# Two gate products of the first chunk moved into the prologue of a fused attention and GLU kernel, its last keys in halves, its statistics divided anew

## The chip, the core and the metric

The kernel runs on one core of a Trainium2 chip. The metric is the device time of one execution in microseconds (us), the median of three runs. The core's engines work through lists of instructions of their own, in order, and wait for each other with semaphores: TensorE (PE in the profile, PEld its weight loads), VectorE (DVE), ScalarE (ACT), GpSimd (POOL), and SyncE (SP), which here only issues transfers (DMA). PE writes its results into PSUM, a memory of eight banks of 2 KB for each of 128 partitions; all else is in SBUF.

## The reference

The input x has 2048 tokens of 640 values; weights and data are bf16. Two branches share the layer norm of x:

```python
xn = (x - mean) / sqrt(var + 1e-5)
# attention, 32 heads of 20
q, k, v = split(xn @ wqkv)
s = softmax(q @ k.T * 20 ** -0.5) @ v @ wo
# gated linear unit, F = 1728
h = sigmoid(xn @ w_gate) * (xn @ w_up)
g = silu(h @ w_down)
out = x + s * g
```

## The kernel before, in words

The queries are cut into four chunks of 512 tokens (`QC`), the heads into eight groups of four (`GH`); a block is one group with one chunk of queries. The program has two stages, and in both the Python code works out an order of instructions ahead of time from assumed costs, by a clock of its own (`t` in the first, `now` in the second). The chip then runs each engine's list in that order; nothing is reordered there.

**The prologue** (L199 to L401) loads 16 tiles of 128 tokens of x and makes from them the transposed, normalised input `xnT`, and the keys, queries and values that the first block needs. Its pieces are `Step` objects with a cost on each engine that may run them, predecessors, and a key: at each time an engine takes the ready step with the largest length of work behind it (`order()`) less its `late`. For each tile:

- `s_stats` takes mean and variance, on DVE (two statistics instructions and one to join them) or on ACT (two passes with sums, L269 and L270); `ACT_STATS` lists the tiles that ACT has, here eight. `X_AT` is the time from which a tile is assumed to be there.
- `s_rstd` takes the inverse root on POOL, for `RH` tiles at once; for tiles of ACT it also corrects the mean (L279).
- `s_xn` normalises on DVE, `s_tr` transposes on PE in five pieces into a PSUM buffer `tp`, and `s_ev` copies that into `xnT` on ACT or DVE, whichever is free (L295).

For each chunk, `s_k` multiplies the keys of the first head group into the PSUM bank `pk`, `s_kmax` takes their largest absolute value per row on DVE, `s_kt` copies them out. `s_q`, `s_abs`, `s_bound` and `s_qev` make the queries of the first block: an upper bound of each row's scores, from the maxima of all four chunks, is subtracted by a matmul (`q_bound`), so that the exponentials need no running maximum. So the first scores wait for the maximum of the last chunk's keys. `s_v` and `s_vev` make values for the first two chunks (`NVP`). Where PE has nothing ready, it gets a scrap matmul (L398) on a tile `busy` and a bank `scrap` of its own, whose result nobody reads.

**The main stage** (L1160 to L1500) simulates PE, ACT and DVE in steps of 0.02 us and emits what they would take next. Score tiles of 128 keys by 512 queries are filled by PE (`score_mm`, L889). ACT turns most into exponentials (`exp_act` over `act_imm`, L82: pairs into `pt`, single ones into `px`). DVE does the others with integer arithmetic: it reads the scores into `iv` (L1327) and makes three passes over four such tiles into `pb` (L1019, L1022, L1025); a DVE tile goes through PE's second product twice. `oacc` (L926) sums the weighted values. Everything else is an `Item` that fills gaps: keys, queries and values for later groups, then `glu_items`, in order, which hold the whole GLU. For each chunk `mk_gu` makes 14 column tiles: a gate product, tanh on ACT (L82, output `tnh`), an up product, and on DVE (tanh + 1) × up into `hT` (L690). The last column tile is half as wide and is handled apart. Then `mk_down` multiplies `hT` with `wd`. All these PE products go by `cols` (L471), four matmuls on four column strips of the array at once.

**Transfers.** The order of SP's transfers isn't written out: they are put where their buffers come free. `load_wgu(c, k2)` (L425) loads gate and up weights of two column tiles, 320 KB each, into one of two buffers. The first such load, the output weights `wo` and the down weights `wd` stand in the code at the start of the main stage (L1161 to L1170), with two small POOL memsets of `wd` and `hT`. The pools `late` (`wd`, `wo`, `hT`) and `w2` (the weights `wgu` and all buffers of the main stage) are opened after the prologue's pool `lp` is closed, on the same memory. The small weights of the second head group (`load_wst`, spread on POOL by L128) are loaded during the prologue.

## Time and profile before

The median of three runs is 803.62 us (802.97 to 803.87). The profiled execution took 803.38 us, of which its span, first to last instruction, is 801.6; the mean granted clock of TensorE was 0.997.

| Stretch, us | length | PE busy | DVE busy | ACT busy | POOL busy | what |
|---|---|---|---|---|---|---|
| 0 to 4 | 4 | 2.69 | 0.79 | 2.36 | 3.10 | first tiles land, scrap matmuls |
| 4 to 8 | 4 | 1.31 | 2.86 | 3.94 | 3.55 | statistics |
| 8 to 12 | 4 | 3.61 | 3.70 | 2.56 | 3.58 | first transposes |
| 16 to 18 | 2 | 2.00 | 2.00 | 1.97 | 1.56 | middle of the prologue |
| 24 to 26 | 2 | 1.99 | 1.49 | 1.51 | 0 | last transposes |
| 26 to 28 | 2 | 1.83 | 0.85 | 0.34 | 0 | last keys |
| 28 to 30 | 2 | 1.01 | 1.22 | 0.51 | 0.95 | bound, first scores |
| 30 to 34 | 4 | 3.10 | 2.64 | 3.84 | 0.99 | main stage begins |
| 130 to 330 | 200 | 196.87 | 196.98 | 199.89 | 15.69 | middle of the main stage |
| 790 to 796 | 6 | 6.00 | 3.84 | 0.74 | 1.63 | last output tiles |

DMA is busy until 14.2 us, then nearly idle to 29, and busy again to 42 (0.96 to 1.08 of the 16 engines).

How to read a row of the profile: in a list of instructions in order of time, the columns are start, duration (of all that the line merges), engine, source line, operation, output <- inputs, shapes, count; in square brackets the idle time of the engine before it, and whose end it waited for by the profile. A matmul's duration includes its way through the array, so rows that follow each other overlap: what one costs is read from start to start. The scrap matmuls count as busy PE.

### The profile page before, as it was taken

What the parts mean: (1) busy time and instruction counts of PE and PEld (TensorE: products, weight loads), DVE (VectorE), ACT (ScalarE), POOL (GpSimd) and SP (SyncE); (2) the same over time, 40 slices, a digit from 0 to 9 for tenths busy, and PEclk for the clock granted to TensorE, in tenths of its full rate; (3) what the DMA queues carried; (4) which work ended last, traced back from release to release, by engine and by line L of the source; (5) the groups of instructions that cost most, each with busy time, mean ns of one, the idle gap of its engine ahead of it and who ended that gap; (6) DMA issues with size and microseconds to landing.
All of it is one profiled execution on the core that took longest, in us unless ns stands there. A gap on an engine that the chain in (4) does not pass through costs nothing.

```text
span 801.6 us, 25395 instructions
## 1 busy us (share of the span) xinstructions
PE 778.0 (97%) x10462; PEld 283.8 (35%) x10466; DVE 770.2 (96%) x1239; ACT 781.2 (97%) x991; POOL 107.4 (13%) x219
## 2 busy tenths in 40 slices
PE   7899999999999999999999999999999999999996
PEld 5523233333433323334332332334333333333333
DVE  7798999999999999989999999999999999999996
ACT  8799999999999999999999999999999999999993
POOL 7200000000000000000000010000000100502425
PEclk9999999999999999999999999999999999999999
DMA  5541213123122323222113132222311332331421
GB/s 162 147 117 48 70 40 86 53 67 80 46 69 61 78 67 100 51 60 68 49 47 97 50 86 76 80 75 60 96 40 58 91 90 53 105 104 34 131 62 62
DMA packets 91851, 60.47 MB, mean 75 GB/s; under 512 B 34891, under 2 KB 85627, under 8 KB 91735
## 3 DMA queue, kind: packets, MB, share of 16 engines
q1 hardware_dynamic: 91447, 58.52, 26.2%
q8 instruction: 82, 1.34, 0.7%
q14 instruction: 34, 0.28, 0.1%
q10 hardware_dynamic: 288, 0.33, 0.1%
HBM read 45.18 MB, written 11.09 MB: 70 GB/s over the span
## 4 chain that ended last, share of the span: by engine, by line
PE 47%; ACT 39%; DVE 6%; issue 5%; DMA 1%; POOL 1%; DVEq 0%; ACTq 0%; POOLq 0%; SPq 0%
ACT pt L82 31%; PE bk L473 20%; PE scA L889 14%; PE oacc L926 10%; ACT px L82 4%; DVE iv L1327 2%; ACT tnh L82 2%; DVE pb L1025 1%; PE bk L889 1%; ACT td L82 1%; DVE pb L1022 1%; PE tp L292 1%; DVE pb L1019 0%; DMA lt<-ld 0%; ACT aq L173 0%
## 5 line engine op out<-in xcount | busy, mean ns | idle before, releaser
L82 ACT ACTIVATE pt<-scA 128x1024 bf16<-128x1024 f32 (+1 forms) x709 | 707.8, 1186 | 1.2 <-PE scA L889 0.5
L1327 DVE TENSOR_SCALAR iv<-bk 128x512 int16<-128x512 f32 x500 | 331.5, 680 | 12.1 <-PE bk L889 9.6
L889 PE MATMUL scA<-q,kT 32*128 32x512 bf16 x1412 | 275.8, 382 | 8.7 <-ACT pt L82 3.3
L889 PE MATMUL bk<-q,kT 32*128 32x512 bf16 x636 | 207.3, 383 | 0.2 <-DVE iv L1327 0.2
L889 PEld LDWEIGHTS <-kT 32*128 32x128 bf16 x2048 | 88.4, 91 | 262.0 <-issue 250.7
L926 PE MATMUL oacc<-pt,v 128*21 128x512 bf16 x1412 | 178.6, 381 | 1.0 <-ACT pt L82 0.7
L926 PE MATMUL oacc<-pb,v 128*21 128x512 bf16 x1000 | 161.4, 382 | 0.0
L473 PE MATMUL bk<-xnT,wgu 128*32 128x512 bf16 x2160 | 157.3, 383 | 0.5 <-DVE iv L1327 0.2
L1025 DVE TENSOR_TENSOR pb<-iv,pb 128x2048 bf16<-128x2048 bf16 x125 | 152.0, 1216 | 0.7
L979 POOL TENSOR_TENSOR on_bf<-on,rl 128x128 bf16<-128x128 f32 x116 | 54.4, 473 | 626.7 <-DVE iv L1327 149.1
L82 ACT ACTIVATE px<-bk 128x512 bf16<-128x512 f32 x136 | 101.0, 760 | 1.7 <-POOL hT L1169 1.6
L1019 DVE TENSOR_SCALAR pb<-iv 128x2048 int16<-128x2048 int16 x125 | 86.9, 695 | 0.4
L473 PE MATMUL bk<-wd,hT 128*32 128x320 bf16 x1792 | 87.0, 302 | 0.1
L1022 DVE TENSOR_SCALAR pb<-iv 128x2048 int16<-128x2048 int16 x125 | 86.2, 690 | 0.0
L926 PEld LDWEIGHTS <-v 128*21 128x21 bf16 x2548 | 54.0, 91 | 76.2 <-issue 53.4
L473 PEld LDWEIGHTS <-wgu 128*32 128x32 bf16 x2160 | 44.5, 95 | 64.3 <-issue 45.9
L473 PEld LDWEIGHTS <-hT 128*32 128x32 bf16 x1792 | 37.5, 95 | 38.2 <-issue 32.7
L473 PE MATMUL bk<-xnT,wu 128*32 128x512 bf16 x640 | 48.4, 383 | 0.6 <-DVE iv L1327 0.2
L926 PE MATMUL oacc<-px,v 128*21 128x512 bf16 x136 | 46.7, 381 | 0.0
L82 ACT ACTIVATE tnh<-bk 128x512 bf16<-128x512 f32 (+1 forms) x56 | 43.2, 772 | 0.1
L690 DVE SCALAR_TENSOR_TENSOR hT<-tnh,bk 128x512 bf16<-128x512 bf16 x52 | 35.3, 679 | 1.0 <-PE bk L889 0.3
L800 POOL TENSOR_TENSOR xnT<-otmp,xnT 128x160 bf16<-128x160 f32 x48 | 28.2, 607 | 40.6 <-PE bk L889 15.9
(118 smaller groups left out, 410.5 us busy)
## 6 DMA issues: line engine op xcount, KB each, us to landing
rl<-rd SPq DMA_DIRECT2D x124, 64.0 KB
wgu<-in_B_w_gate_dram SPq DMA_DIRECT2D x24, 320.0 KB
wgu<-in_B_w_up_dram SPq DMA_DIRECT2D x24, 320.0 KB
gq_dram<-gqs SPq DMA_DIRECT2D x24, 160.0 KB
xnT<-gq_dram SPq DMA_DIRECT2D x12, 320.0 KB
xt<-in_A_x_dram SPq DMA_DIRECT2D x16, 160.0 KB
xnT<-in_A_x_dram SPq DMA_DIRECT2D x16, 160.0 KB
out_dram<-xnT SPq DMA_DIRECT2D x14, 160.0 KB
```

What stands on the lines that cost most here:

```text
L82: return nc.scalar.add_instruction(mybir.InstActivation(func=func, name=nc.get_next_instruction_name(), engine=ENG.Activation, ins=[nc.sca ...
L292: nc.tensor.transpose(out=tps[k][:, kd, :], in_=xns[k][:, kd * P:(kd + 1) * P], identity=ident)
L473: nc.tensor.matmul(out[j:j + 32, :], lhsT=lhsT[:, j:j + 32], rhs=rhs, start=start, stop=stop, tile_position=(0, j), skip_group_check=True)
L690: return nc.vector.scalar_tensor_tensor(out=hT[0:fs, kf, :], in0=st["t"][0:fs, :], scalar=1.0, in1=st["u"][0:fs, :], op0=ALU.add, op1=ALU. ...
L800: add = nc.gpsimd.tensor_tensor(out=xr[:, cs], in0=tmp[:, i * HD // 2:(i + 1) * HD // 2], in1=xr[:, cs], op=ALU.add)
L889: nc.tensor.matmul(dst, lhsT=kTs[gc_of(b)[0] % 2][32 * j:32 * j + 32, kt * P:(kt + 1) * P], rhs=qts[b % 3][32 * j:32 * j + 32, :], start=T ...
L926: nc.tensor.matmul(oacc[32 * j:32 * j + DH + 1, :], lhsT=lhsT, rhs=u["src"], start=first, stop=last, tile_position=(0, 32 * j), skip_group ...
L979: ins = nc.gpsimd.tensor_tensor(out=on_bf[:, cs], in0=on[:, cs], in1=rl[:, cs], op=ALU.mult)
L1019: ins = nc.vector.tensor_scalar(out=pb[:, 0, :, :].bitcast(I16), in0=iv, scalar1=0x7F80, scalar2=1, op0=ALU.bitwise_and, op1=ALU.bitwise_or)
L1022: ins = nc.vector.tensor_scalar(out=pb[:, 1, :, :].bitcast(I16), in0=iv, scalar1=0x007F, scalar2=0x3F00, op0=ALU.bitwise_and, op1=ALU.bitw ...
L1025: ins = nc.vector.tensor_tensor(out=pb[:, 1, :, :], in0=iv.bitcast(BF16), in1=pb[:, 1, :, :], op=ALU.mult)
L1327: beat(nc.vector.tensor_scalar(out=d["iv"][:, j, :], in0=bank[bk], scalar1=B_OFF, scalar2=0.0, op0=ALU.add, op1=ALU.max))
```

## The change

Five things change, nearly all in the prologue.

1. **Gates of the first chunk.** The gate products of the first two column tiles (`NGP = 2`; `NHP = 0`: no product with the up part) are multiplied in the prologue, with full-width matmuls in three steps each, from planned time 14.0 (`G_AT`) on and with low rank (`L_G`); tanh of them goes straight into `hT[:, 0]` and `hT[:, 1]`. In the main stage `mk_gu` returns only the up item for these two, and its DVE product reads `hT` in place.
2. **Weights and memory.** The pools `late` and a new `wg` (weights `wgu`, `tnh`, `gql`) are opened before the prologue. The first gate and up weights are loaded right behind the value weights, the second pair at the start of the main stage, and the load that the first up item started is left out.
3. **Last keys in two halves.** `KP` splits the key product and the maximum of the fourth chunk in 256 columns each; the tile of maxima has room for eight, five are used.
4. **Statistics.** ACT keeps tiles 2, 4, 10 and 12; DVE has the other twelve. The offsets `L_*` of the ranks change, and `EARLY` adds to the rank of five single steps.
5. **PSUM and scrap.** Transposes have three buffers where they had four, values (with the gates and the scrap bank) share three where values had one and scrap one. Scrap matmuls stop at planned time 13.0 (`T_SCR`).

```diff
-    def k_max(g, c, src=None):
+    def k_max(g, c, src=None, n=NQC):
         if not mk_n.setdefault(g, []):
-            mks[g] = wk.tile([P, NQC], FP32, tag="mk4", bufs=2, name="mk4")
+            mks[g] = wk.tile([P, 2 * NQC], FP32, tag="mk4", bufs=2, name="mk4")
...
-            nc.vector.tensor_reduce(out=mk, in_=mks[g], axis=AXISX, op=ALU.max)
+            nc.vector.tensor_reduce(out=mk, in_=mks[g][:, 0:n], axis=AXISX, op=ALU.max)
...
+    late = ctx.enter_context(tc.tile_pool(name="late", bufs=1))
+    wg = ctx.enter_context(tc.tile_pool(name="wg", bufs=2))
+    wd = late.tile([P, NFT, D], BF16, name="wd", tag="wd")
+    wo = late.tile([P, KD, D], BF16, name="wo")
+    hT = late.tile([P, NFT, QC], BF16, name="hT")
...
+    NGP, NHP = 2, 0
     NVP = 2
-    RH = 2
+    RH = (2, 2, 2, 2)
+    KP = [[(0, 4)], [(0, 4)], [(0, 4)], [(0, 2), (2, 4)]]
+    EARLY = {('stats', 15): 4.0, ('stats', 12): 2.0, ('ev', 6): -1.0, ('kt', 2): 4.0, ('k', 1, 0): 8.0}
...
-    L_ST, L_CH, L_K, L_V, L_Q = 4.0, 1.5, 10.0, 3.0, 2.0
-    ACT_STATS = (0, 2, 4, 7, 8, 10, 11, 12)
+    G_AT, L_G, NPV, T_SCR = 14.0, 11.0, 3, 13.0
+    L_ST, L_CH, L_K, L_V, L_Q = 3.0, 2.0, 7.0, 7.0, 0.5
+    ACT_STATS = (2, 4, 10, 12)
...
         wv0 = load_wv(0)
+        for k2 in range((NGP + 1) // 2):
+            load_wgu(0, k2)
...
-            tps[k] = psP.tile([P, KD, P], BF16, tag="tp", bufs=4, name="tp")
+            tps[k] = psP.tile([P, KD, P], BF16, tag="tp", bufs=3, name="tp")
...
-        def s_k(eng, c):
-            pks[c] = psP.tile([P, 512], FP32, tag="pk", bufs=1, name="psk")
-            k_mm(pks[c], 0, c)
+        def s_k(eng, c, lo, hi):
+            if lo == 0:
+                pks[c] = psP.tile([P, 512], FP32, tag="pk", bufs=1, name="psk")
+            q = slice(lo * P, hi * P)
+            for kd in range(KD):
+                nc.tensor.matmul(pks[c][:, q], lhsT=wslice(0, 1, kd), rhs=xnT[:, c, kd, q],
+                                 start=(kd == 0), stop=(kd == KD - 1))
...
+        def s_gu(eng, kf, i, lo):
+            if lo == 0:
+                gus[(kf, i)] = psP.tile([P, 512], FP32, tag="pv", bufs=NPV, name="psg")
+            for kd in range(lo, min(KD, lo + 2)):
+                nc.tensor.matmul(gus[(kf, i)], lhsT=wgu_tiles[(0, kf // 2)][:, i, kd, kf % 2 * P:kf % 2 * P + P],
+                                 rhs=xnT[:, 0, kd, :], start=(kd == 0), stop=(kd == KD - 1))
+
+        def s_th(eng, kf):
+            act_imm(hT[:, kf, :], gus[(kf, 0)], ACT.Tanh, 0.5)
...
+            for lo, hi in KP[c]:
+                km = Step(s_k, (c, lo, hi), {"PE": 0.04 + 0.27 * (hi - lo)}, (spread, *evs[4 * c + lo:4 * c + hi], *mine[-1:]),
+                          take=None if lo else "pk", late=L_CH * c + L_K)
+                mine.append(km)
+                kms.append(Step(s_kmax, (c, lo, hi), {"DVE": 0.08 + 0.14 * (hi - lo)}, (km, *kms[-1:]), late=L_CH * c))
...
+        hs = []
+        for kf in range(NGP):
+            for i in range(2 if kf < NHP else 1):
+                for lo in range(0, KD, 2):
+                    g = Step(s_gu, (kf, i, lo), {"PE": 0.44 if lo < 4 else 0.22}, (*evs[0:4], *hs[-1:]), G_AT, take=None if lo else "pv", late=L_G)
+                    hs.append(g)
+                if i == 0:
+                    th = Step(s_th, (kf,), {"ACT": 0.48}, (g,), give="pv", late=L_G)
...
-        scrap = psP.tile([P, 512], FP32, tag="scrap", bufs=1, name="scrap")
+        scrap = psP.tile([P, 512], FP32, tag="pv", bufs=NPV, name="scrap")
...
-                    s = max(can, key=lambda s: s.order() - s.late)
+                    s = max(can, key=lambda s: s.order() - s.late + EARLY.get((s.f.__name__[2:],) + s.args[0:2], 0.0))
...
-                elif e == "PE" and engs[e] <= t:
+                elif e == "PE" and engs[e] <= t < T_SCR:
...
-            if ko == 0:
+            if ko == 0 and not early:
...
+            t = hT[:, kf, :] if early else st["t"]
+            return nc.vector.scalar_tensor_tensor(out=hT[0:fs, kf, :], in0=t[0:fs, :], scalar=1.0,
                                                   in1=st["u"][0:fs, :], op0=ALU.add, op1=ALU.mult)
...
+        return pair[1:] if early else pair
...
-        load_wgu(0, 0)
+        load_wgu(0, (NGP + 1) // 2)
```

## The prediction

> **What bounds the kernel now.** I read the page first (span, engine shares), then the busy time by stage, then the prologue in order of time with the waits in it, and the granted clock there microsecond by microsecond.
>
> ```profile
> span 801.6 us, 25395 instructions
> PE 778.0 (97%) x10462; PEld 283.8 (35%) x10466; DVE 770.2 (96%) x1239; ACT 781.2 (97%) x991; POOL 107.4 (13%) x219
> ```
>
> Three engines look equally full. The stages tell them apart (columns: stretch, length, busy time of PE, PEld, DVE, ACT, POOL, clock, DMA):
>
> ```profile
> 24.00:26.00 2.00, 1.99 (x28) 1.73 (x27) 1.49 (x3) 1.51 (x3) 0.00 (x0) 1.00 0.00 0
> 26.00:28.00 2.00, 1.83 (x12) 0.97 (x10) 0.85 (x2) 0.34 (x2) 0.00 (x0) 1.00 0.00 0
> 28.00:30.00 2.00, 1.01 (x10) 0.36 (x10) 1.22 (x3) 0.51 (x1) 0.95 (x2) 1.00 0.00 0
> 130.00:330.00 200.00, 196.87 (x2636) 68.90 (x2625) 196.98 (x314) 199.89 (x251) 15.69 (x35) 1.00 0.26 70
> 330.00:530.00 200.00, 196.81 (x2636) 68.44 (x2636) 194.42 (x306) 199.89 (x249) 14.44 (x32) 1.00 0.24 66
> ```
>
> From 42 us on ACT is busy 99.9% of the time, DVE and PE a little less: the main stage lasts as long as ACT's list, and DVE shares the exponentials. Before it ACT is nearly empty from 26 to 30 us. What it waits for is a chain (start, duration, what):
>
> ```profile
> 24.82 0.88 DVE L295 COPY xnT<-tp 128x640 bf16<-128x640 bf16 x2
> 25.82 1.24 PE L142 MATMUL psk<-xnT,wqk 128*128 128x512 bf16 x5
> 27.10 0.69 DVE L158 TENSOR_REDUCE mk<-psk 128x1 f32<-128x512 f32 x1 [1.40 <-PE psk L142]
> 27.83 0.16 DVE L162 TENSOR_REDUCE mk<-mk 128x1 f32<-128x4 f32 x1
> 28.02 0.25 DVE L163 TENSOR_SCALAR md<-esum,mk 128x128 bf16<-128x128 bf16 x1
> 28.76 0.69 DVE L180 TENSOR_SCALAR q<-psq 128x512 bf16<-128x512 f32 x1 [0.48 <-PE psq L177]
> 30.16 0.60 ACT L82 ACTIVATE px<-bk 128x512 bf16<-128x512 f32 x1 [1.64 <-POOL hT L1169]
> ```
>
> The last copy out of PSUM ends at 25.70, the maximum of the last keys starts at 27.10, and the first exponential at 30.16. The bracket on that last line names POOL, but DVE's first read of scores starts at 30.12, so the scores (started at 29.60) explain 30.16 too. Before 25.70, DVE works from 3.58 on with 1.59 us of named waits: it is the fuller engine of the prologue.
>
> **The change part by part.** Durations are start to start, since rows overlap.
>
> *Main stage.* Two gate products and two tanh leave. ACT: a tanh starts at 44.40, the next instruction at 44.88, and 52.43 to 52.90: 0.48 each, 0.95 together. If DVE cannot take less, ACT's list shortens by 0.95. If the split is rebalanced: eight exponentials of 1024 take 52.43 − 44.88 = 7.55, so 0.47 a score tile on ACT; on DVE a tile costs 0.60 (from 45.37 to 45.97, one 512-wide read of PSUM to the next) and a quarter of three passes (0.60 + 0.60 + 1.13), 1.18. Rates 2.12 and 0.85 a us: 0.95 × 2.12 / 2.97 = 0.68. PE: 40 matmuls in groups of four that run together; twenty ran from 42.72 to 43.92, the start of the next fill, 1.2 each gate. A freed PE also feeds DVE, which waited 10 us for score tiles over the stage (group of that read: 10.2 before it). So 0.68 at least, 2.4 if PE alone were the bound, 0.68 being nearest to ACT's 99.9%; I take 1.0. Any new order of the whole stage may move ±1.
>
> *Last keys in two halves.* The first half (tiles 12 and 13) is multiplied and reduced before the last copy ends. After that copy remain five 256-wide matmuls and a 256-wide maximum. Before: 1.40 from copy to maximum, then 0.73 to the next reduction. The five matmuls were 1.24; half the columns save about 0.5 (0.62 if all halves, nothing if fixed). The maximum: 0.60 start to start, of which half less a fixed 0.08, about 0.3. Saved 0.8, from 0.4 to 0.9. The extra reduction costs DVE 0.36, counted next. The 8-wide maxima tile, reduced over 5 instead of 4, stays at 0.16.
>
> *Statistics.* Four tiles go from ACT (1.69, from 12.46 to 14.15) to DVE (1.04, 8.60 to 9.64). DVE until its last copy: 12 × 1.04 + 16 normalisations × 0.34 + 3 maxima × 0.60 + 0.36 = 20.1, and 0.41 a copy that it makes. It can start at 3.1 (the first tile's arrival, when ACT started). ACT, from 4.9 (tile 2 lands): 4 × 1.69 + absolute value 0.48 + three key copies 0.58 + some 1.4 of values and tanh, and 0.62 for each of the other copies: 20.3 − 0.62n, n being DVE's copies. Equal where 23.2 + 0.41n = 25.2 − 0.62n: n = 2, 24.0. With about 1.2 of waits and issue gaps (DVE had 1.6 named), 25.2 against 25.70: 0.5 saved, between 1.0 and −0.4. It is nearer to the first because the ACT-first copies now find ACT free. POOL's fix-ups of the mean (0.19 a tile) fall from 8 to 4; POOL has slack.
>
> *Gates and tanh in the prologue.* PE: 2 × 5 full-width matmuls, 1.24 a set by the row of the query product; they lie in the time that scrap matmuls filled (16.5 to 18.2). tanh: 2 × 0.48 on ACT; ACT stands 3.3 us idle between 25.70 and 30.16, so nothing; without that cover 0.95. No table row but the one at 0.80 us exists although tanh and exponentials alternate, so no table load. The in-place product on DVE stays in the main stage at 0.60.
>
> *Queues.* SP: the first gate and up weights (640 KB) move from 29.08 to just behind the value weights (9.76), past the second head group's small weights; the next 640 KB, the output and down weights (2.1 MB) no longer share memory with the prologue's buffers and may follow at once. SP waits in order, but DMA is idle from 14.2 to 29. The gates need the first 320 KB: before, 3.24 MB had moved by 14.2; at its 270 GB/s that is about 14.7 to 15.9, against planned 14.0. PE would wait, with transposes behind it and DVE copies behind them: up to 1.9, but PE reached its comparable filler only at 16.5, so 0. POOL's two clearings (0.63 and 0.52 at 29.05) lose their wait on the last scrap matmul: 0 to −0.15, since scores end where they did. The second group's weight spread behind them is used later: 0. The main stage's exponential buffers now lie on the prologue's memory; its last readers there are transposes, done by 24.8, before any score: 0. The in-place product waits for a tanh made long before: 0.
>
> *PSUM.* Transposes get 3 buffers, not 4. Around 15.4 four copies stood in a row, so a fourth transpose may wait one copy, 0 to 0.4; I take 0.1, inside the 1.2 of waits above. Values get 3 buffers for 1: 0 to −0.3, taken 0. The moved order keys (second chunk's keys earlier, values later, two statistics earlier): ±0.4, taken 0.
>
> *No scrap after 13 us.* Here the clock must hold by itself:
>
> ```profile
> 7.00:8.00 1.00, 0.00 (x0) 0.00 (x0) 0.97 (x4) 0.97 (x3) 0.77 (x4) 0.95 1.01 237
> 8.00:9.00 1.00, 0.61 (x6) 0.62 (x7) 1.00 (x4) 0.97 (x5) 0.93 (x2) 0.50 0.90 273
> 11.00:12.00 1.00, 1.00 (x14) 0.97 (x13) 0.73 (x2) 0.13 (x1) 0.85 (x3) 0.84 0.90 302
> 799.00:800.00 1.00, 0.00 (x0) 0.00 (x0) 0.00 (x0) 0.00 (x0) 0.00 (x0) 0.90 0.72 265
> ```
>
> PE stops at 5.31 and the clock halves at 7.9; it is back at 11.33; at the end PE stops at 796.5 and the clock halves at 799.8. From 28.4 to 31.8 PE is busy 2.08 of 3.40 and stays at 1.00. With the last keys 0.5, the bound 0.2 and two transposes 0.6, the new 3.4 us before the scores hold some 1.3 to 1.8. Nothing in these rows places 45%; I take it as holding, cost 0, up to 1.9 (below).
>
> [...]
>
> *Sum.* 1.0 + 0.8 + 0.5 = 2.3. The profiled execution took 803.38 (span 801.6, 1.8 around it), so 801.1 for it; the median 803.62 stands 0.24 above: 801.3. Own range of this case: saved at least 0.68 + 0.4 + 0 = 1.1, at most 1.2 + 0.9 + 1.0 = 3.1, so 800.5 to 802.5.
>
> **The rivals.**
>
> *PE binds the main stage.* For it: PE 98% busy. Against: its busy ends are modelled, and ACT's 99.9% leaves no room. Then 2.4 + 1.3 = 3.7 saved: 799.9. Chance 0.12.
>
> *The clock halves before the main stage.* The first 3.4 us of scores run at half speed; PE had 2.08 of work there in 3.4, so at half it needs 4.2, and 0.8 to 2.1 is lost; I take 1.9, leaving 0.4: 803.2. [...] Chance 0.16, the case of no measurable change.
>
> *DVE becomes the prologue's bound (other side).* Place: the copies out of PSUM. Each copy that falls to DVE costs 0.41; DVE's own list is then 23.2 + 0.41n + 1.2 of waits. Gain ends where it passes 25.70 + 0.8 + 1.0 = 27.5, n = 7.6. With ten copies, as before, and two statistics (1.04 each; DVE runs in order) ahead of the last chunk's copies, it is 28.5 + 2.1 = 30.6, 3.1 past that: 806.7. For it: DVE is already the fuller engine. Against: ACT loses 6.8 of statistics and takes copies first. Chance 0.22.
>
> **How the numbers follow.** A measurement tells about 0.2%, 1.6 us: faster is under 802.0, slower over 805.2. Forecast 0.50, PE 0.12: faster 0.62. Clock 0.16: same. DVE 0.22: slower. The time is the likeliest case's, 801.3. The range goes down to 799.8, past the PE case, and up to 805.4, to the nearer half of the DVE case; that leaves out some 0.05 below and 0.12 above.
>
> **What would show it.** The last copy near 25.2 with 2 to 4 of 16 on DVE; from there to the first exponential 3.7 instead of 4.46, so that exponential near 28.8; 54 tanh from the scores on, ACT still 99.9% busy; clock 1.00 from 11.3 to 33; weights landed by 28 us. I am wrong if PE stands waiting for the gate weights after 15, if the clock reads 0.5 near 29, if DVE copies eight tiles or more, or if the main stage gets longer from its new order.

## The result

The changed kernel takes 810.89 us (median; 810.02 to 812.12). The kernel before, on the same chip, took 803.75 (802.97 to 804.11). The ratio is 1.0085, with a 95% interval from 1.0073 to 1.0098: slower by 7.1 us. The forecast was 801.3 with a range from 799.8 to 805.4: the time moved the other way, and past the range.

The profiled execution took 812.12 us, at the upper end of its runs, with a span of 810.4 and a mean clock of 0.987 (before: 803.38, 801.6 and 0.997). The page opens like this:

```profile
span 810.4 us, 25266 instructions
PE 777.7 (96%) x10416; PEld 284.3 (35%) x10416; DVE 772.0 (95%) x1244; ACT 780.2 (96%) x981; POOL 107.0 (13%) x215
```

ACT has 1.0 us less work than before and the span is 8.8 longer: the loss is waiting, not work. ACT's list, from its first exponential to its last, tells where it lies:

| us | before | after | difference |
|---|---|---|---|
| first exponential starts | 30.16 | 32.68 | +2.52 |
| ACT idle, from there to 740 | 0.57 | 2.25 | +1.68 |
| ACT idle, from 740 to its last exponential | 0.73 | 5.97 | +5.24 |
| ACT busy between first and last exponential | 757.64 | 757.77 | +0.13 |
| after the last exponential | 12.55 | 11.73 | −0.82 |
| sum | | | +8.75 |

The two tanh did leave (54 instead of 56), but ACT took one score tile more (1549 instead of 1548), so its busy time is the same: −0.97 for the tanh, +1.11 for two more instructions of two tiles and three fewer of one. The end is 0.82 shorter, but that can't be put to the gates: a later run without them (e13_prologue12) has 11.87 there. Three waits make up the loss. The busy time by stretch shows the second and third (columns: stretch, length, busy time of PE, PEld, DVE, ACT and POOL, granted clock, DMA share, GB/s), and in its first row a part of the first:

```profile
8.00:12.00 4.00, 2.85 (x20) 2.42 (x21) 3.32 (x8) 1.71 (x4) 3.57 (x10) 0.50 0.93 283
30.00:34.00 4.00, 2.10 (x14) 1.00 (x15) 3.09 (x5) 1.85 (x3) 0.61 (x1) 0.68 0.00 0
34.00:38.00 4.00, 4.00 (x28) 2.43 (x25) 1.35 (x2) 3.53 (x5) 0.00 (x0) 0.50 0.02 6
755.00:760.00 5.00, 0.87 (x18) 0.24 (x12) 0.90 (x3) 2.21 (x3) 0.00 (x0) 0.85 0.35 103
760.00:765.00 5.00, 5.00 (x56) 1.63 (x55) 3.81 (x6) 2.54 (x3) 2.06 (x5) 0.50 0.64 185
```

Two such rows of the kernel before:

```profile
34.00:38.00 4.00, 3.80 (x43) 1.96 (x46) 3.46 (x7) 4.00 (x6) 0.00 (x0) 1.00 1.05 276
740.00:760.00 20.00, 19.71 (x324) 7.80 (x320) 19.33 (x34) 19.73 (x26) 8.47 (x16) 1.00 0.45 139
```

Before, the stretch from 34 to 38 had a clock of 1.00 and 43 matmuls, with PE 3.80 us busy. Now PE is "full" with 28, because each takes longer: a busy share at half clock is not a share of work done. From 755 to 760 PE, DVE and ACT mostly stand still together; before, ACT was busy for 19.73 of the 20 us from 740 to 760.

**First wait: the prologue.** The list in order of time (start, duration, what; in brackets the engine's idle time before it, and whose end it waited for):

```profile
3.26 0.52 POOL L1218 MEMSET hT<- 64x512 bf16 x1
7.58 0.23 POOL L302 TENSOR_SCALAR rstd<-mv 128x2 f32<-128x2 f32 x1
8.65 0.81 DVE L313 TENSOR_SCALAR xn<-xt,mv,rstd 128x640 bf16<-128x640 bf16 x2 [1.10 <-POOL rstd L304]
9.15 1.25 PE L320 MATMUL tp<-ident,xn 128*128 128x128 bf16 x10 [4.02 <-DVE xn L313]
27.50 0.49 DVE L323 COPY xnT<-tp 128x640 bf16<-128x640 bf16 x1 [0.18 <-PE tp L320]
28.14 0.42 DVE L159 TENSOR_REDUCE mk<-psk 128x1 f32<-128x256 f32 x1
28.62 0.72 PE L331 MATMUL psk<-xnT,wqk 128*128 128x256 bf16 x5 [0.30 <-DVE mk L159]
29.38 0.42 DVE L159 TENSOR_REDUCE mk<-psk 128x1 f32<-128x256 f32 x1 [0.81 <-PE psk L331]
29.76 0.85 POOL L128 COPY wqk<-wst 128x800 bf16<-128x800 bf16 x1 [4.78 <-DMA wst<-in_A_wqkv_dram]
29.84 0.16 DVE L163 TENSOR_REDUCE mk<-mk 128x1 f32<-128x5 f32 x1
30.03 0.63 DVE L164 TENSOR_SCALAR md<-esum,mk 128x128 bf16<-128x128 bf16 x1
32.68 0.60 ACT L82 ACTIVATE px<-bk 128x512 bf16<-128x512 f32 x1 [2.15 <-DVE oacc L472]
```

The last copy ends at 27.99, where 25.70 was before and 25.2 was forecast: +2.29 of the +2.52 arose ahead of it. The first row says how that begins. The clearing of `hT`, an instruction of the main stage by its line, runs at 3.26 us, ahead of the first inverse root. The clearing of `wd` (0.63) runs at 2.15. That root starts at 7.58 instead of 6.31, the first normalisation at 8.65 instead of 7.92, and PE stands for 4.02 us instead of 3.07. In the kernel before:

```profile
6.31 0.23 POOL L274 TENSOR_SCALAR rstd<-mv 128x2 f32<-128x2 f32 x1
7.92 0.77 DVE L285 TENSOR_SCALAR xn<-xt,mv,rstd 128x640 bf16<-128x640 bf16 x2
```

The clock is then at 0.50 until about 14.4 (before: until 11.33), and the scrap matmuls in PE's list, planned at 0.14 each, take 0.21 each, start to start, ahead of the query product and the later transposes (seven from 10.19 to 11.68, eight from 12.75 to 14.41).

**Third wait: the stall near 755,** the largest:

```profile
749.26 0.67 DVE L1008 COPY on<-oacc 128x512 f32<-128x512 f32 x1
749.76 3.04 SPq L1058 DMA_DIRECT2D oU<-on_bf  x4
753.43 0.56 SPq L1010 DMA_DIRECT2D ld<-on  x1
755.25 0.33 SPq L1012 DMA_DIRECT2D lt<-ld  x1
759.10 0.25 DVE L1018 RECIPROCAL rt<-lt 128x16 f32<-128x16 f32 x1 [4.24 <-DMA lt<-ld]
759.96 0.60 PE L975 MATMUL oacc<-pb,v 128*21 128x512 bf16 x3 [4.13 <-DVE pb L1068]
761.60 0.60 ACT L82 ACTIVATE px<-bk 128x512 bf16<-128x512 f32 x1 [4.39 <-PE bk L938]
```

After a block's sums are copied out, the row sums travel through memory: SP sends `on` to `ld`, then `ld` to `lt`, and DVE takes the reciprocal. Here `ld` stands on SP's queue behind four transfers of the block before, which start when POOL is done (749.70) and take 3.04 to issue, and behind a load of x (752.90); it leaves 4.2 us after its copy began. DVE's list has the reciprocal in a fixed place, so DVE stands 4.24 us; its exponentials are missing for PE, and PE's scores for ACT. PE's pause is followed by a fall of the clock, at 758.5, to 0.50 until about 765, which costs ACT two more waits, 0.45 and 0.96. Before, the same path took 6.66 us from copy to reciprocal instead of 9.84, and DVE waited 0.67 there:

```profile
746.17 0.68 DVE L959 COPY on<-oacc 128x512 f32<-128x512 f32 x1
748.63 0.56 SPq L961 DMA_DIRECT2D ld<-on  x1
750.62 0.33 SPq L963 DMA_DIRECT2D lt<-ld  x1
752.83 0.25 DVE L969 RECIPROCAL rt<-lt 128x16 f32<-128x16 f32 x1 [0.67 <-DMA lt<-ld]
```

Of the 3.18 more, 1.71 lie before `ld` leaves and 1.64 between `lt` and the reciprocal (3.85 instead of 2.21), less 0.17 between the two transfers.

### The profile page after: what moved, and what is told of

It is laid out like the page before. It is cut to its first block, busy times and chain, and to the rows that moved or that the text cites. A ratio compares the mean times of both kernels' runs of the same rounds, so it can differ in the third digit from the quotient of the medians.

```text
span 810.4 us, 25266 instructions
## 1 busy us (share of the span) xinstructions
PE 777.7 (96%) x10416; PEld 284.3 (35%) x10416; DVE 772.0 (95%) x1244; ACT 780.2 (96%) x981; POOL 107.0 (13%) x215
## 4 chain that ended last, share of the span: by engine, by line
ACT 49%; PE 34%; DVE 8%; issue 7%; POOL 1%; DMA 1%; DVEq 0%; ACTq 0%; POOLq 0%
ACT pt L82 39%; PE bk L515 14%; PE scA L938 11%; PE oacc L975 6%; ACT px L82 5%; DVE iv L1376 3%; ACT tnh L82 2%; DVE pb L1074 1%; ACT td L82 1%; DVE pb L1068 1%; PE bk L696 1%; DVE pb L1071 1%; ACT xnT L323 1%; PE bk L938 1%; DVE hT L734 0%
## 5 line engine op out<-in xcount | busy, mean ns | idle before, releaser
L975 PE MATMUL oacc<-pt,v 128*21 128x512 bf16 x1416 | 184.8, 382 | 0.1
L515 PE MATMUL bk<-xnT,wgu 128*32 128x512 bf16 x2120 | 155.2, 383 | 0.7
L1074 DVE TENSOR_TENSOR pb<-iv,pb 128x2048 bf16<-128x2048 bf16 (+1 forms) x125 | 152.6, 1221 | 0.8
L1068 DVE TENSOR_SCALAR pb<-iv 128x2048 int16<-128x2048 int16 (+1 forms) x125 | 87.0, 696 | 1.0
L1071 DVE TENSOR_SCALAR pb<-iv 128x2048 int16<-128x2048 int16 (+1 forms) x125 | 86.1, 689 | 0.0
L515 PE MATMUL bk<-wd,hT 128*32 128x320 bf16 x1792 | 85.0, 302 | 0.6 <-ACT px L82 0.4
L82 ACT ACTIVATE tnh<-bk 128x512 bf16<-128x512 f32 (+1 forms) x54 | 40.9, 757 | 0.1
L845 POOL TENSOR_TENSOR xnT<-otmp,xnT 128x160 bf16<-128x160 f32 x48 | 29.9, 642 | 39.8 <-DVE otmp L840 22.6
```

The costliest lines, as they stand in the source:

```text
L82: return nc.scalar.add_instruction(mybir.InstActivation(func=func, name=nc.get_next_instruction_name(), engine=ENG.Activation, ins=[nc.sca ...
L515: nc.tensor.matmul(out[j:j + 32, :], lhsT=lhsT[:, j:j + 32], rhs=rhs, start=start, stop=stop, tile_position=(0, j), skip_group_check=True)
L845: add = nc.gpsimd.tensor_tensor(out=xr[:, cs], in0=tmp[:, i * HD // 2:(i + 1) * HD // 2], in1=xr[:, cs], op=ALU.add)
L975: nc.tensor.matmul(oacc[32 * j:32 * j + DH + 1, :], lhsT=lhsT, rhs=u["src"], start=first, stop=last, tile_position=(0, 32 * j), skip_group ...
L1068: ins = nc.vector.tensor_scalar(out=pb[:, 0, :, :].bitcast(I16), in0=iv, scalar1=0x7F80, scalar2=1, op0=ALU.bitwise_and, op1=ALU.bitwise_or)
L1071: ins = nc.vector.tensor_scalar(out=pb[:, 1, :, :].bitcast(I16), in0=iv, scalar1=0x007F, scalar2=0x3F00, op0=ALU.bitwise_and, op1=ALU.bitw ...
```

## The experiments

The theory from the changed kernel's trace had three causes: clearings (POOL), clock, and the late stall. The rivals were that the gates, the halves or the division of the statistics cost the time themselves. One table for all runs; "idle" is ACT's between its first and last exponential, up to 740 us and after, and the ratio is to the kernel before, timed beside it (a median of 803.8 to 804.2).

| run | first exponential | idle to 740 | idle after | median us | ratio (95%) |
|---|---|---|---|---|---|
| before | 30.16 | 0.57 | 0.73 | 803.75 | |
| after | 32.68 | 2.25 | 5.97 | 810.89 | 1.0085 (1.0073 to 1.0098) |
| e1_clears_late | 30.36 | 2.44 | 4.33 | 809.00 | 1.0067 (1.0047 to 1.0088) |
| e2_scrap_kept | 32.62 | 1.17 | 2.78 | 809.29 | 1.0065 (1.0050 to 1.0080) |
| e3_no_gates | 31.93 | 2.07 | 0.12 | 806.85 | 1.0038 (1.0024 to 1.0052) |
| e4_clears_scrap | 31.27 | 1.15 | 3.25 | 808.07 | 1.0052 (1.0037 to 1.0067) |
| e5_late_norm | 33.26 | 1.14 | 0.94 | 805.86 | 1.0030 (1.0020 to 1.0040) |
| e6_gates_alone | 34.39 | 1.25 | 3.62 | 809.69 | 1.0075 (1.0059 to 1.0092) |
| e7_gates_late_norm | 34.27 | 1.24 | 0.83 | 807.24 | 1.0042 (1.0027 to 1.0057) |
| e8_two_banks | 31.49 | 1.17 | 4.46 | 809.37 | 1.0073 (1.0057 to 1.0090) |
| e9_warm | 31.60 | 1.12 | 1.77 | 807.52 | 1.0043 (1.0029 to 1.0057) |
| e10_before_warm | 29.98 | 0.59 | 2.64 | 805.40 | 1.0011 (1.0002 to 1.0021) |
| e11_prologue_warm | 31.76 | 0.78 | 0.84 | 805.88 | 1.0018 (1.0009 to 1.0028) |
| e12_warm12 | 31.28 | 1.14 | 1.39 | 805.04 | 1.0015 (1.0004 to 1.0027) |
| e13_prologue12 | 31.19 | 0.76 | 0.76 | 806.22 | 1.0033 (1.0018 to 1.0047) |
| e14_old_stats | 31.03 | 0.57 | 2.19 | 805.90 | 1.0022 (1.0013 to 1.0032) |

### One cause at a time

**The clearings behind the prologue.** They are emitted after the prologue's list, with everything else as changed.

```diff
-            nc.gpsimd.memset(wd[fsz[-1]:P, nfull, :], 0.0)
-            nc.gpsimd.memset(hT[fsz[-1]:P, nfull, :], 0.0)
...
+        nc.gpsimd.memset(wd[fsz[-1]:P, F // P, :], 0.0)
+        nc.gpsimd.memset(hT[fsz[-1]:P, F // P, :], 0.0)
```

> The changed kernel, with POOL's two clearings (of the down weights' and the hidden tile's unused rows, 0.63 and 0.52 us) put behind the last inverse root of the prologue in POOL's list, instead of ahead of the first. Theory POOL (the clearings, freed from their wait, cut into the prologue and delay the first normalisation from 7.92 to 8.65): the first inverse root moves from 7.58 to about 6.4, the 1.1 us that VectorE waited for it go, the first exponential comes at 31.4 to 31.9 instead of 32.68, and the time is 0.8 to 1.3 below the changed kernel's 810.9: about 809.8. Rival DVE list (the prologue is as long as VectorE's list and the wait is made up later): first exponential within 0.3 of 32.68, time 810.5 to 811. The late wait of 4.2 us in VectorE near 755 stays by both, since the main stage's order is untouched.

The time fell by 1.9 us to 809.00, though its runs (807.51 to 811.24) overlap with those of the changed kernel (810.02 to 812.12). The first inverse root is back where it was, and the first exponential nearly:

```profile
6.30 0.23 POOL L302 TENSOR_SCALAR rstd<-mv 128x2 f32<-128x2 f32 x1
30.36 0.60 ACT L82 ACTIVATE px<-bk 128x512 bf16<-128x512 f32 x1 [1.56 <-PE bk L940]
```

So the clearings are the cause of the late root. The 2.32 at the first exponential are not all theirs: in this profile the clock was 1.00 from 6.7 us, where its record begins, to 30.6. That is luck, for with the clearings in the same late place two later profiles had it lower and a first exponential of 31.27 and 33.26 (below). So what the clearings alone cost the first exponential is not shown. The rest of the loss, idle time of 2.44 and 4.33, is untouched.

**Scrap matmuls to the end of the prologue.** Scrap has its own bank again, values and gates share two.

```diff
-    G_AT, L_G, NPV, T_SCR = 14.0, 11.0, 3, 13.0
+    G_AT, L_G, NPV, T_SCR = 14.0, 11.0, 2, 1e9
...
-        scrap = psP.tile([P, 512], FP32, tag="pv", bufs=NPV, name="scrap")
+        scrap = psP.tile([P, 512], FP32, tag="scrap", bufs=1, name="scrap")
```

> The changed kernel, with scrap matmuls to the end of the prologue on a bank of their own (two buffers for values and gates instead of three). Theory clock (without scrap the tail holds too little work, the clock halves at 31.3 and the main stage starts at half speed until 38): clock 1.00 from 31 to 38, the 1.07 us that ScalarE waited for scores between 34 and 39 go, time 1.0 to 1.5 below 810.9: about 809.6. Rival (the start of the main stage is limited by the engines' lists, PE has slack there): clock 1.00 but the time within 0.4 of 810.9. First exponential within 0.3 of 32.68 by both.

The time fell by 1.6 to 809.29. Two microseconds at the start of the main stage by the busy time, in this run:

```profile
34.00:36.00 2.00, 1.87 (x22) 1.27 (x21) 1.26 (x2) 2.00 (x4) 0.00 (x0) 1.00 0.01 4
```

The same two in the changed kernel, whose first exponential is as late (32.68, here 32.62):

```profile
34.00:36.00 2.00, 2.00 (x16) 1.13 (x13) 0.54 (x1) 1.68 (x4) 0.00 (x0) 0.50 0.04 12
```

With scrap the clock is 1.00, ACT is full and PE gets 22 matmuls done; without it the clock is 0.50, PE does 16, and ACT waits. ACT's idle time up to 740 fell from 2.25 to 1.17. So the clock at the start of the main stage costs about 1.1 us directly. A run further down agrees: e8_two_banks gives no late scrap either, but its clock happened to hold, and it was idle for 1.17. The late stall shrank too (5.97 to 2.78), without having been touched: `ld` still left 4.16 us after its copy, but from `lt` to the reciprocal it was 2.44 instead of 3.85.

**No gates in the prologue.** The main stage then has the work, and so the planned order, of before.

```diff
-    NGP, NHP = 2, 0
+    NGP, NHP = 0, 0
```

> The changed kernel with no gate in the prologue: the main stage then has the list of the kernel before, all else of the change stays. Theory order (the new list of the main stage puts a short transfer of row sums behind others in SP's list, VectorE waits 4.2 us for it near 755, PE and ScalarE stand behind, and the clock halves): no such wait, ScalarE's idle time from 700 to 790 falls from 6 to under 1 us, two more tanh cost 0.95, time about 810.9 - 6 + 0.9 = 805.8, between 805 and 807.2. Rival prologue (all of the loss is made before 40 us): time 810.5 to 812. Rival gates (the in-place product or the early tanh is what costs): the wait near 755 stays.

806.85, 4.0 less than the changed kernel: the largest single step. Little of it is the prologue: its first exponential is at 31.93, 0.75 earlier, and the idle time up to 740 is still 2.07. Most is the stall, which is gone (idle after 740: 0.12). The waits of the reciprocal in DVE's list from 690 to 790 us (columns: total, count, longest), in the changed kernel:

```profile
DVE rt L1018 <- DMA lt<-ld: 4.2, 1, 4.2
```

And in this run:

```profile
DVE rt L1018 <- DMA lt<-ld: 1.1, 2, 0.8
```

Taking two gates out of the main stage reordered it 700 us later, and one row-sum path met a busy queue. That is still "the order" as a whole; the next pair tests the path itself.

### The causes together, and the stall by itself

> Both mends of the first two runs together. Theory POOL and theory clock independent: first exponential at 31.4 to 31.9, clock 1.00 from there on, time 810.9 - 1.1 - 1.2 = 808.6. If one cause hides the other (scrap matmuls keep the clock, so that the delay by POOL no longer starts a halved window between 8 and 14), the gain is that of the larger one alone: about 809.6.

Both first edits together gave 808.07, 2.8 less than the changed kernel, where the two alone gave 1.9 and 1.6, 3.5 in sum; with each kernel's runs 1.5 to 4 us apart, the difference is not resolved. The stall is still there (2.4).

Then one constant on top of it: `T_L2` is the delay that the planner assumes from the copy of the sums to the reciprocal, for the last blocks. Nothing else of the code is changed: the reciprocal is put later in DVE's list, and the planner shifts what stands around it.

```diff
-    LATE, T_LT, T_OU, T_L2, T_RL = 1.0, 9.0, 1.5, 4.5, 5.6
+    LATE, T_LT, T_OU, T_L2, T_RL = 1.0, 9.0, 1.5, 7.0, 5.6
```

> The run with both mends (808.07), and in the planned order the reciprocal of the row sums of the last blocks comes 7.0 instead of 4.5 us after their copy (T_L2). Theory order: VectorE's wait of 2.4 us for that transfer near 755 and the waits of ScalarE behind it (4.5 us in that run, 6 in the changed kernel) shrink below 1, time 3 to 4 below: about 804.6. Rival (the wait is only moved, since what is late is the row sums' way through SP's list, or other transfers take its place): a wait of 2 us or more stays after 740, time within 1 of 808.1.

805.86: 2.2 less, although the first exponential of this profile is 2 us later. The wait of the reciprocal fell from 2.4 to this:

```profile
DVE rt L1020 <- DMA lt<-ld: 0.6, 1, 0.6
```

So the stall is the planned delay of 4.5 us against a path that took 6.2 to 9.8 in the blocks where DVE waited over 0.2 us for it. With 7.0 it took 9.0 to 10.1 in one block of each such run, and DVE still waited 0.4 to 2.0 there: the constant makes the stall smaller and does not end it. The two runs have the same prologue, instruction for instruction, and yet a first exponential at 31.27 and 33.26. The clock tells them apart: 0.59 from 8 to 12 us and 1.00 from 12 to 16 in the first, 0.50 and 0.69 in the second. In the second, DVE waited 0.58 us for inputs where it had not waited in the first, and the first transposes came at 8.50 instead of 7.87. In the traces before and after the change the shorter stretches at one clock last 3.41 us (7.91 to 11.32 before), twice that (7.54 to 14.36 after) or five times that (14.36 to 31.43 after), so stretches of 3.41 are compared. In the second run PE was busy for 2.58 of the 3.41 us from 7.67 to 11.08, and the clock stayed at 0.50; in the first run it was busy for all of 7.88 to 11.29, and the clock came back. As far as these two profiles show, a small delay of the inputs becomes 2 us by way of the clock.

### Which part of the change carries the rest

**The gates with the old keys, statistics, ranks and four transposition buffers,** with the clearings late and scrap kept, then with the later reciprocal:

```diff
-    KP = [[(0, 4)], [(0, 4)], [(0, 4)], [(0, 2), (2, 4)]]
+    KP = [[(0, 4)], [(0, 4)], [(0, 4)], [(0, 4)]]
...
-    G_AT, L_G, NPV, T_SCR = 14.0, 11.0, 3, 13.0
+    G_AT, L_G, NPV, T_SCR = 14.0, 11.0, 1, 1e9
...
-    ACT_STATS = (2, 4, 10, 12)
+    ACT_STATS = (0, 2, 4, 7, 8, 10, 11, 12)
```

> The kernel before, with only the two gates and their tanh in the prologue (the weights and the pools moved as they must be, POOL's clearings put behind the prologue's work); statistics, ranks, PSUM buffers, scrap and the whole last keys as before. Theory gates-by-order: first exponential within 0.5 of 30.16, the wait near 755 is there, main stage without it 1 to 2 us shorter; time 803.75 + 4.4 - 1.5 = 806.6, between 805.5 and 807.5. Rival statistics (the new division and ranks are what costs): 802 to 803.5, no wait near 755. Rival prologue gates (they sit in the way of transposes and keys): first exponential over 31.

> The run of the gates alone, with the reciprocal 7.0 instead of 4.5 us after the copy. Theory order: the wait near 755 goes, time 803.75 - 1.5 = 802.3, between 801.5 and 803.3, faster than the kernel before. Rival (moving tanh gains nothing, or the wait only moves): 804 or more.

809.69 and 807.24. The first exponential is at 34.3 to 34.4 in both, the latest of all. But there values and gates had one PSUM buffer for both, and the gates piled up behind it at the end of the prologue: ACT waited 4.1 us for them, and PE was still full of them from 28 to 30. This is what gates in the prologue cost with one buffer; it says nothing of the changed kernel, which has three. What the pair does show is the stall again: the constant alone gave 2.45 us (809.69 to 807.24), with idle time after 740 from 3.62 to 0.83. And it shows what the freed gates are worth: from its first exponential to its end the second run takes 771.5 us, and the kernel before takes as much.

**The halves in two banks.** The second half of the last keys gets a bank of its own, on top of the first run's edit; values and gates have two buffers instead of three for it, and the last keys are copied out in two pieces.

```diff
+            elif c == NQC - 1:
+                pks[c, 1] = psP.tile([P, 512], FP32, tag="pk2", bufs=1, name="psk2")
...
-                nc.tensor.matmul(pks[c][:, q], lhsT=wslice(0, 1, kd), rhs=xnT[:, c, kd, q],
+                nc.tensor.matmul(pks[c, 1][:, q] if lo else pks[c][:, q], lhsT=wslice(0, 1, kd), rhs=xnT[:, c, kd, q],
```

> The run with the clearings late (809.0), with the second half of the last keys in a PSUM bank of its own (two buffers for values and gates instead of three). Theory bank: in the changed kernel the second half's matmuls wait for VectorE's maximum of the first half, though both columns are different (0.30 and 0.69 us before them on PE and its weight loads); here they start within 0.2 of the last copy's end, and from that copy's end to the joint maximum it is 1.2 instead of 1.75 to 1.85. Rival order (they wait because of PE's list): 1.7 or more. The time moves by 0.5 or less, within the spread of either.

In the changed kernel the second half's matmuls wait for DVE's maximum of the first half (28.62, "0.30 <-DVE mk"), though it reads other columns. With two banks all ten matmuls run in one go and that wait is gone:

```profile
27.31 1.43 PE L333 MATMUL psk<-xnT,wqk 128*128 128x256 bf16 x10
28.06 0.42 DVE L159 TENSOR_REDUCE mk<-psk 128x1 f32<-128x256 f32 x1 [0.62 <-PE psk L333]
28.78 0.42 DVE L159 TENSOR_REDUCE mk<-psk 128x1 f32<-128x256 f32 x1 [0.30 <-PE psk L333]
```

But the first half is no earlier: its maximum starts at 28.06, after the last copy (27.99), as it did in the changed kernel (28.14). So the split still can't hide the first maximum behind the last copy. But from last copy to joint maximum it is 1.25, as the theory had it, where the first run had 1.87: sharing costs 0.62 there. Whether it is the bank or the tile that the program's semaphores go by was not tried. The run without gates shows the same bond from the other side. There both halves were multiplied in one go into one bank, and the maximum of the first half had to wait for both:

```profile
27.39 1.36 PE L331 MATMUL psk<-xnT,wqk 128*128 128x256 bf16 x10
28.78 0.76 DVE L159 TENSOR_REDUCE mk<-psk 128x1 f32<-128x256 f32 x2 [0.81 <-PE psk L331]
```

The time did not fall with two banks (809.37 against 809.00): the last copy came at 27.99 instead of 26.24, with a clock of 0.50 from 9.6 to 13.0 and another order in DVE's list. A miss as a repair.

### The clock at the start, and what is left of the prologue

PE gets scrap matmuls ahead of its planned list, so that its first pause is shorter: 30 on the run with the later reciprocal, 30 on the kernel before, 30 without gates. The question is whether the first exponential then comes as early as in e1_clears_late (30.36), whose record has the clock at 1.00 all through the prologue from 6.7 on.

```diff
+        for _ in range(30):
+            nc.tensor.matmul(scrap[:, 0:2 * P], lhsT=busy[:, 0:P], rhs=busy, start=True, stop=True)
```

> The run with the late reciprocal (805.9), and 30 more scrap matmuls at the start of PE's list, which fill the gap of 3 to 4 us before the first transposes. [...] Rival (gates, statistics or PSUM buffers make the prologue long whatever the clock): first exponential 31.2 or later, time 805 or more.

> The kernel before with the same 30 scrap matmuls. Theory: it loses to the halved clock between 8 and 11.3 as well, but little, since its statistics on two engines keep VectorE busy: first exponential 29.5 to 30.1 against 30.16, time 803.0 to 803.7. Rival (the scrap delays the first transposes): 804 to 805.

> The first of these runs without the gates: all of the new prologue but for them, warm, with the clearings late. Theory: the gates cost the prologue little when it is warm (0.3 to 0.8: they stand ahead of the last transposes and the second half of the last keys), so the first exponential comes at 29.6 to 30.3; the main stage has the two tanh again. Rival (the gates are what makes the prologue long): 1.5 us or more earlier than with them. Time 802.5 to 804.

Thirty were too many in the new prologue: PE worked on scrap until 9.7 us, so the first transposes came at 9.71 and 9.82, later than in the changed kernel (9.15). With gates, 23 scraps from 2.78 us on took 0.21 us each, and the next 21, from 7.42 on, 0.12; the record of the clock begins at 7.13. So a clock of 1.00 that the profile shows ahead of its first record is not measured. The runs show two things all the same. With gates (31.60) and without (31.76) the first exponential is equally late, so the gates cost the prologue nothing. And the kernel before, with a first exponential 0.2 earlier than in its own profile, became slower by 0.11%: ACT's idle time after 740 rose from 0.73 to 2.64, with a clock of 0.50 from 755.3 to 758.7, as its own waits for `lt` from 700 to 790 us rose from 1.5 to this:

```profile
DVE rt L971 <- DMA lt<-ld: 2.5, 2, 1.6
```

The tight transfer was in the old kernel too; how long it stalls moves with what goes before. The later reciprocal was not tried on the old kernel.

Then twelve instead of thirty: with gates, without them, and without them with the old eight statistics on ACT.

```diff
-    ACT_STATS = (2, 4, 10, 12)
+    ACT_STATS = (0, 2, 4, 7, 8, 10, 11, 12)
```

> The run with the late reciprocal (805.9), and 12 instead of 30 more scrap matmuls at the start, so that they end before the first normalised tile is there (30 held the first transposes back to 9.71). Theory clock: the clock stays 1.00 from 5 to 16, the first transposes start at 7.9 to 8.6, the first exponential comes at 30.2 to 30.9, time 803.3 to 804.6. Rival lists (the new prologue is longer than the old one, warm or not): first exponential 31.2 or later, time 805 or more.

> The same without the gates. With the gates free of cost in the prologue, as two warm runs showed (31.60 with, 31.76 without), the first exponential is within 0.4 of that of the run with gates. If they do cost, it is 0.7 or more earlier.

> The prologue without gates and 12 more scrap matmuls, with the statistics divided as before (eight tiles on ScalarE, eight on VectorE). Theory statistics (twelve tiles on VectorE make its list the bound): first exponential 0.7 or more earlier than with four on ScalarE. Theory balance (moving four tiles and as many copies the other way changes little, as the prediction had it): within 0.5, or later.

With twelve the clock is 1.00 from its first record (6.2 to 6.8 us) to the end of the prologue, and the first transposes start at 8.73, 8.39 and 8.57. The first exponentials are at 31.28, 31.19 and 31.03. So gates cost this prologue 0.1, and even with the clock at 1.00 it is about 1.1 us longer than the old (30.16). The last pair splits this. The last copy out of PSUM ends at 27.19 (with gates), 27.08 (without) and 25.90 (old division): with two buffers for values and gates, the new division delays the last copy by 1.2 us, where 0.5 was to be saved. That the old division gains only 0.16 at the first exponential is due to the keys:

```profile
25.54 0.69 ACT L150 ACTIVATE kT<-psk,ones_r 128x512 bf16<-128x512 f32 x1
27.02 0.42 DVE L159 TENSOR_REDUCE mk<-psk 128x1 f32<-128x256 f32 x1 [1.12 <-PE psk L331]
28.24 0.42 DVE L159 TENSOR_REDUCE mk<-psk 128x1 f32<-128x256 f32 x1 [0.80 <-PE psk L331]
```

There the third chunk's keys are copied out of the only key bank until 26.23, the first half begins at 26.28, and the two halves follow each other 1.22 us apart. From last copy to the joint maximum (28.70) it takes 2.80 us, against 2.13 in the kernel before with one undivided product.

But these prologues are not quite the change's own. With two buffers instead of three the planner puts a copy ahead of a statistic in DVE's list, in e8_two_banks too, which has no late scrap. The first run (e1_clears_late) kept the change's order of DVE and ACT, with the clock at 1.00 from 6.7 to 30.6, and its last copy came earlier than with twelve scraps, at 26.24:

```profile
25.12 1.12 DVE L323 COPY xnT<-tp 128x640 bf16<-128x640 bf16 x2
```

Its first exponential, 30.36, is only 0.2 later than the old. So of the 1.1 some 0.9 came with the mends, by their order or by the scrap in PE's list. No run joins the change's own order and three buffers with a clock that holds to the end and the later reciprocal.

The version with gates and twelve scraps is the best of the change, 805.04: of the 7.1 us lost, 5.9 came back with the gates, the early weights, the halves and the new division all kept. It does not beat the kernel before (1.0015, from 1.0004 to 1.0027), and no other run does. That the version without gates has less idle time but a longer time (806.22) shows that the last 1 us between such medians doesn't rank these versions: their intervals overlap. With thirty scraps it was the other way, 807.52 with gates and 805.88 without. So no pair shows that moving the gates gained time.

## Why the prediction was wrong

**POOL's clearings: "0 to −0.15", measured 1.27 at the first root.** This step failed first. It took the clearings to stay in their place in the order, only with a shorter wait. Freed of the memory that they shared with the prologue's buffers, they ran near the head of POOL's list instead (2.15 and 3.26), in front of a root that everything in the prologue waits for. Moved back, 1.9 us returned in the median; in that profile the clock was also at 1.00 from 6.7 to 30.6, where the changed kernel had 0.50 from 7.54 to 14.36, and what each gave was not tried apart. What is theirs at the first exponential stays open: it came at 31.93 to 32.68 with the clearings early, and at 30.36 to 33.26 with them late.

**Statistics and last copy: 25.2, measured 27.99, or 26.24 in the change's own order with the clock at 1.00.** The sum for DVE had the right form, and DVE did make 3 of the 16 copies, as worked out. Its terms were too small by 1.0. In the run with the clearings late DVE spent, start to start from 3.19 on: 12.6 on statistics (forecast 12.5), 6.1 on normalisations (5.4, though the list of the kernel before has 6.1 too), 1.5 on three copies (0.82 for two), 1.7 on maxima (2.16 with the first half, which now comes later), 1.1 in waits (1.2). In the changed kernel itself the waits were 1.10 for POOL, 1.56 for key products and 0.18 for transposes, 2.84 together, and they are the other 1.75: the clearings and the halved clock, which no term had. So the rival "DVE becomes the prologue's bound" named the right engine by the wrong route: normalisations and waits, not ten copies, and 1 to 3 us, not 5.

**Last keys in halves: 0.8 saved, measured 0.3 to 0.5 in one bank where it saved, 0.9 in two.** From last copy to joint maximum it was 2.13 before, 1.85 after, 1.60 without gates, 1.75 with twelve scraps, 1.25 with two banks, and 2.80 with the old statistics. The step that failed is "the first half is multiplied and reduced before the last copy ends". In every one of these profiles the first half was reduced after it. In one bank the second half's matmuls then waited for that maximum, and the two maxima start 1.22 to 1.24 us apart; only in e3_no_gates, where both halves were multiplied first, did the first maximum wait instead. The size was right for two banks; the bond of the two halves in one bank was the term left out.

**md, not in the sum: +0.38.** The weight spread of the second group was written off as "used later: 0". Its load now stood behind 4.2 MB on SP's queue (issued at 21.17 instead of 10.78), so it ran at 29.76, beside DVE's `md` step, which took 0.63 instead of 0.25 and ended at 30.66, 0.05 behind POOL's copy (30.61). The two other profiles in which they overlap, scrap kept (30.74 and 30.69) and the later reciprocal (31.38 and 31.33), have the same 0.05. Why DVE's step takes longer beside that copy no run here shows.

**Clock: taken as holding, cost 0; measured 1.1 directly, 1.6 in time.** The rival with a chance of 0.16 was one of the things that happened, and its size (up to 1.9) was fair. The clock was 0.50 from about 31.4 to 38.3. The fall came behind a tail that held key halves, a bound and a gate step: PE was busy for 1.42 of the 3.42 us from 28.01 to 31.43, within the 1.3 to 1.8 that the forecast put there. The two transposes (0.6) that the forecast counted in it were not there: the last ended at 27.5. In the tails without late scrap, stretches with PE busy for 0.90, 1.42 and 1.43 of 3.4 us (e3_no_gates, the changed kernel, e1_clears_late) were followed by half the clock, and the one with 2.34 (e8_two_banks) was not. Near 755, though, two stretches with 2.16 and 2.18 (e14_old_stats, e10_before_warm) were, so the busy share alone does not decide; what does stays open. The forecast had no term for the clock in the prologue, which was at 0.50 until about 14.4 instead of 11.33; the same planned prologue behind twelve scraps, at 1.00, was 2.0 us shorter (31.28 against 33.26).

**Main stage: 1.0 saved, and "any new order may move ±1"; measured nothing saved, and +5.2 in one place.** The step "ACT's list shortens" failed: ACT took a score tile over from DVE, and its list stayed as long (757.77 against 757.64). From the first exponential to the end no profile is shorter than the kernel before, 771.5 us; the best with gates is the same. The margin failed too. It took a new order to shift waits at random by small amounts. But both orders, old and new, plan 4.5 us for a path that took 6.2 or more where DVE waited for it, and one bad meeting costs 4 us and then a halved clock. The late stall and the clock around it make up 5.2 of the 8.8 us of the profiled executions; the prologue 2.5, the clock at the start of the main stage most of 1.7.

**The range.** Its lower sum took 0 for the statistics, where their own range went to −0.4, and left out the ±1 of the main stage's order and the ±0.4 of the prologue's. With them it is a loss of 0.7 and not a gain of 1.1. The output and down weights are 2960 KB together, not the 2.1 MB of the down weights alone; nothing hung on that.

**Right:** no table load beyond the one at 0.79 us, 54 tanh, weights landed by about 28.5, PE never waited for the gate weights (the gates began at 19.07), and the gates cost the mended prologues next to nothing (31.60 against 31.76, and 31.28 against 31.19). In the changed kernel they cost 0.75 (32.68 against 31.93): the last copy is as late, and 0.38 of it is `md`. PE did not bind.

**Open:** with the clock at 1.00, two buffers and the old division the new prologue is still 0.9 us longer than the old. The halves in one bank and the late release of that bank by the third chunk account for 0.67 from last copy to joint maximum; how much of the release is due to the new ranks, the five early steps or three transposition buffers was not tried apart, nor how much of the later last copy is due to the two buffers and how much to the scrap.

## What to carry to other kernels

When memory is laid out anew, look for instructions whose only brake was the shared memory: they run at once (here at 2.15 and 3.26 us instead of 29.05 and 29.62), in the same in-order list as the work that the path needs. In an order planned from assumed delays, list the steps whose real delay is longer than the planned one; any edit, however far away, can turn one of them from hidden to 4 us, and one constant may be worth more than the edit. Splitting a step pays only if the first part really ends earlier, and if the second can be written while the first is being read: here 0.3 us in one bank and 0.9 in two.

## What the runs showed that was not expected

- Two parts of one PSUM bank are not independent here: matmuls into columns 256 to 511 waited 0.30 us for DVE's read of columns 0 to 255 (weight loads 0.69); in a bank of their own they did not. The semaphores are the program's own; what would happen without them no run here shows. The forecast had not counted these waits.
- A 128x128 multiply on DVE took 0.63 us beside a POOL copy of 128x800, and 0.25 or 0.26 in runs where that copy did not overlap it.
- The same prologue, instruction for instruction, ended 2.0 us apart in two profiles, with granted clocks of 0.59 and 1.00 or 0.50 and 0.69 in the same two stretches.
- The kernel before, started 0.2 us earlier, was 0.11% slower (0.02 to 0.21), with waits 700 us later that had grown from 1.5 to 2.5 us in sum and a halved clock behind them.
